# A chunked recurrence on one core: preparation in another order, and chunk products with a block-diagonal operand

## The chip, the cores and the metric

The kernel runs on one core of one Trainium2 chip. The metric is the device time of one execution in microseconds (us), less is better. The median of three runs of the kernel before is 684.5 us (683.43 to 689.24).

## What is computed

`reference` has two stages. The first is a recurrence over 768 steps t for each of 4 x 8 = 32 heads, with a 40 x 40 state S per head:

```
y_t = r_t S
S   = S * w_t  -  (S a_t) b_t^T  +  v_t k_t^T
```

(`w_t` scales the columns; all of r, k, v, w, a, b have 40 elements per head and step.) The second stage takes y, laid out as 4 x 768 x 320, through four causal attention experts of width 64, of which each token adds the two with the largest gate, weighted by a softmax over the two. The change touches the first stage alone.

## The kernel before, in words

**Chunks, units, windows.** The 768 steps are cut in 24 chunks of 32 steps. Heads are worked on eight at a time (a group g of 0 to 3), so a chunk has four *units* and the recurrence 96, `unit(u)` with u = 4 x chunk + g. Four chunks make a *window* (16 units, 128 steps), of which there are NW = 6. Each iteration n of the main loop issues one step of several units: `u` of unit n-1, `g` of n, `y` of n-3, `f` of n-2, `t` of n-6 (every second n), `k` on half of the iterations, `v` of n-1. Their matmuls run on TensorE (PE); ScalarE (ACT) brings most results out of PSUM; VectorE (DVE) applies the mask behind `f` (L398), multiplies the output y by the decay (L419), and for the last chunk of a window scales the state (L413, with the column PC). The state that `y` gives is read by `g` one iteration later, and the masked result of `f` by `y` of the next iteration.

**Preparation.** Before a window starts, each of its four groups needs `prep(i)`, i = 4 x window + g: two scans over the decays on DVE (`a`, L248, writes SUF; `s`, L254, writes SC), a reciprocal between them (`c`, L252), ScalarE's copy of four columns of SUF into PC (`b`, L250), the scaled a (`x`, L256, writes AA), the scaled k and b (`k` and `l` on DVE, L261, or `p` on GpSimd (POOL), L258, write KB), the products of AA and KB per chunk on PE (`m` for chunks 0 and 1, `n` for 2 and 3, L275), their masks on DVE (L278, into GL), two copies of AA into GL (`d`, `q`, L265 or L267), and a store of part of GL to DRAM (`o`, L282). `w`, `v`, `e` load the next group's inputs.

**Products.** One product is 40 rows of KB x 64 columns against 40 rows of AA x 32 columns, two heads at the array positions (0,0) and (64,64): 32 products per group.

**Inversion.** `invert(w)` loads the stored blocks (`L`), sets their diagonal (`C`), does 30 elimination steps of two instructions each (`T5` is five instructions; on POOL, L309, for window 0 a shorter form on DVE), and transposes (`A`, `B`, `D`, `E`, L311; `P`, L313). For window 0 the two halves are joined by matmuls (`F`, L320, and `H`, L328).

**What sets the order.** Every engine works its own instructions in program order, and that order is written by hand: `START` is the prologue, `EARLY` and the tables `SIDE`, `SIDE2`, `INV`, `INV1` say at which iteration, relative to the window's first, and at which slot (the number of slashes; three put a job behind `f`) which job is issued. Work for window W of `SIDE` is issued one to two windows ahead, -16 being the first iteration of window W-2. In the program before, groups 0 to 4 and the start of 5 are prepared in `START`, the rest of 5, and 6 and 7, in the first iterations of `EARLY`, and the groups of window 2 by `SIDE2` beside the units of window 0.

All PSUM tiles named `ps` come from one ring of four buffers that `u`, `g`, `f`, `v` and the products share.

Of the kernel before, what the change touches and what calls it, by code (L numbers as in the profile page):

```python
# [17 lines left out]
NW, NG, C = 6, 4, 32  # L18
NKB = 10

START = """Z0 E4 0abcsxkl E5 E7 E6 1apb 0m 0d 0q 0n 0o 1csx W2 2apb 1m 1d 1q 1n 1o W4 2csx 3apb 2m 2d 2q 2n 2o W0 W1 V00 V10
3csx 4apb 3m 3d 3q 3n 3o L W3 4csx W5 W6 5apbc 4m 4n C V01 V11 k0 g0 4o Z1 4d 4q T28 A B P F0 5s H0 5x 6apb"""
EARLY = {
    0: "///6cs",
    1: "5mno///6x 7apb/F1",
    2: "6mno///7csx/H1",
    3: "7mno E8",
    4: "/F2/5d/5q",
    5: "/H2/6d/6q",
    6: "/F3/7d/7q",  # L30
    7: "/H3",
}

SIDE = {
    -16: "///0abc",
    -15: "///0sx///0wv",
    -14: "///0k",
    -13: "///0l 1abc///0e",
    -12: "///0m 1s///1w",
    -11: "///1xkl///1ve",  # L40
    -10: "///2abc 1m",
    -9: "///2sx///2wv",
    -8: "///2kl///2e",
    -7: "///3abc 2m",
    -6: "///3sx///3wv",
    -5: "///3k",
    -4: "///3l 0ndqo///3e",
    -3: "///3m 1ndqo",
    -2: "///2ndqo",
    -1: "///3ndqo",  # L50
}

SIDE2 = {
    -13: "///0abc",
    -12: "///0sx///0wv",
    -11: "///0kl 1abc///0e",
    -10: "///1sx///1wv",
    -9: "///0m 1kl///1e",
    -8: "///2abc 1m",
    -7: "///2sxk///2wv",  # L60
    -6: "///2l 3abc///2e",
    -5: "///2m 3sx///3wv",
    -4: "///3kl 0ndqo///3e",
    -3: "///3m 1ndqo",
    -2: "///2ndqo",
    -1: "///3ndqo",
}
INV = {0: "L", 1: "C T5", 2: "T5", 3: "T5", 4: "T5", 5: "T5", 6: "T5", 7: "T5", 8: "T5", 9: "T5", 10: "T5///A", 11: "T5", 12: "T5", 14: "///D", 16: "E"}
INV1 = {4: "L", 5: "C T5", 6: "T5", 7: "T5", 8: "T5", 9: "T5", 10: "T5", 11: "T8", 12: "T8///A", 13: "T8", 14: "T8", 15: "///D", 16: "E"}


def layouts(r, k, v, w, a, b):
# [47 lines left out]
def recurrence(tc, ctx, I, xT, CM, early, tail=None):  # L120
    nc = tc.nc
    ep = early.enter_context(tc.tile_pool(name="early", bufs=1, side="right"))
# [3 lines left out]
    V, A, T, PL = nc.vector, nc.scalar, nc.tensor, nc.gpsimd  # L126
# [17 lines left out]
    SUF = ring("SUF", [104, 529], 1)[0]  # L144
    PC2 = ring("PC", [104, 2, 4], 6)
    SC2 = ring("SC", [104, 2, 16, 33], 6)
    PC, SC = ([t[k // 2][:, k % 2] for k in range(12)] for t in (PC2, SC2))
    KB = ring("KB", [128, 16, 64], NKB)
    AAr = [ep.tile([104, 16, 32], F32, name=f"AA{k}") for k in range(4)]
    GF = [ep.tile([128, 4098], F32, name="GLe")] + ring("GL", [128, 4098], 1)  # L150
    GL = [t[:, 0:4096].rearrange("p (g n s t) -> p g n s t", g=4, n=16, s=2) for t in GF]
    MT = ring("MT", [128, 32, 32], 2)
    RB1 = [ep.tile([128, 8, 32], F32, name=f"RB1{k}") for k in range(2)]
    P1 = ep.tile([128, 32, 16], F32, name="P1")
    EA7 = ep.tile([104, 512], F32, name="EA7")
# [8 lines left out]
    XT = ring("XT", [104, 8, 128], 2)  # L164
# [3 lines left out]
    flat = lambda t: t.rearrange("p a b -> p (a b)")  # L168
# [3 lines left out]
    own = (EWr[0], EAr[0], EKr[0])  # L172
    thirds = lambda t: (t[:, 0:528], t[:, 528:1040], t[:, 1040:2064])
    E8 = [own, thirds(r20), (flat(SC[11]), flat(LS[1])[:, 0:512], g1[:, 0:1024]), thirds(r21),
          (flat(SC[8]), flat(XT[1][:, 4:8]), flat(KB[8])), (flat(SC[9]), flat(XT[1][:, 0:4]), flat(KB[9])), own, (flat(SC[10]), EA7, flat(TT[1]))]

    SUFs = SUF, flat(TT[0])[0:104, 0:529]

# [33 lines left out]
    def rest(x):  # L212
# [19 lines left out]
        else:  # L232
            for k in range(2):
                for b in range(4):
                    q = slice(32 * b, 32 * b + 32)
                    A.activation(RB1[k][q, :, 16:32], ident[q, None, 32 * b + 16:32 * b + 32].to_broadcast([32, 8, 16]), AF.Copy)

    def prep(i):

        w, g = divmod(i, NG)  # L240
        aa, sc, kb, pc = AAr[i % 4], SC[i % 12], KB[i % NKB], PC[i % 12]
        gl = GL[w % 2]
        SUF = SUFs[1 if i in (1, 3, 5) else 0]
        sv = SUF[:, 1:529].rearrange("p (n c) -> p n c", c=33)
        EW, EA, EK = (x[0:104] for x in (E8[i] if i < 8 else own))
        ea = EA.rearrange("p (n c) -> p n c", c=32)
        def f0a():
            V.tensor_tensor_scan(SUF[:, 0:528][:, ::-1], EW[:, ::-1], d1[:, ::-1], 1.0, op0=OP.mult, op1=OP.add)  # L248
        def f0b():
            A.activation(pc, sv[:, ::4, 0], AF.Copy)  # L250
        def f0c():
            V.reciprocal(D1P[:, 0:528:132], sv[:, ::4, 0])  # L252
        def f1():
            V.tensor_tensor_scan(sc.rearrange("p n c -> p (n c)"), EW, D1P, 0.0, op0=OP.mult, op1=OP.add)  # L254
        def f2():
            V.tensor_tensor(aa, ea, sc[:, :, 0:32], op=OP.mult)  # L256
        def fp():
            PL.tensor_tensor(kb[0:104].rearrange("p n (k c) -> p n k c", k=2), EK.rearrange("p (n k c) -> p n k c", n=16, k=2),  # L258
                             sv[:, :, None, 1:33].to_broadcast([104, 16, 2, 32]), op=OP.mult)
        def fk(k):  # L260
            V.tensor_tensor(kb[0:104, :, 32 * k:32 * k + 32], EK.rearrange("p (n k c) -> p n k c", n=16, k=2)[:, :, k], sv[:, :, 1:33], op=OP.mult)  # L261
        def f5(s):
            o, x = gl[64:104, g, :, s, :], aa[64 * s:64 * s + 40]
            if i < 8:
                A.activation(o, x, AF.Copy)  # L265
            else:
                V.tensor_copy(o, x)  # L267
# [178 lines left out]
    P = [prep(i) for i in range(24)]  # L446
# [5 lines left out]
    for W in range(1, NW):  # L452
        n0 = 16 * (W - 1)
        inv = invert(W)
        for r, line in (SIDE if W != 2 else SIDE2).items():
            if W == 1:
                break
            for k, part in enumerate(line.split("/")):
                for z in part.split():
                    at(n0 + r, k, *[P[4 * W + int(z[0])][x] for x in z[1:]])  # L460
        for r, line in (INV1 if W == 1 else INV).items():
            for k, part in enumerate(line.split("/")):
                for z in part.split():
                    at(n0 + r, k, lambda z=z, inv=inv: inv[z[0]](*[int(x) for x in [z[1:]] if x]))
# [37 lines left out]
    for n in range(NU + 4):  # L502
# [468 lines left out]
```

## Time and profile before

| | |
|---|---|
| three runs, median (lowest to highest) | 684.5 us (683.43 to 689.24) |
| profiled execution | 682.19 us |
| its span, first to last instruction | 680.0 us |
| mean granted TensorE clock, share of full speed | 0.907 |
| busy: PE, DVE, ACT, POOL | 593.9, 493.1, 474.3, 321.0 us |
| recurrence (before the attention stage's own units) | about 430 of the 680 us |

A busy time counts an engine's instructions without its waits. Matmuls are pipelined, so PE's busy time is not PE at its peak. The span falls into stages that differ in what is late: a prologue in which few units run, four windows with preparation beside the units (0 to 3), two with little of it (4 and 5), and the attention stage. It is therefore read in stretches. A stretch ends here where the `f` matmuls of a unit start, since those of unit n-2 mark iteration n.

### The profile page before, as it was taken

To read this page: it belongs to the slowest core of one execution; us is meant where nothing else is said; L and a number is where in the kernel's file an instruction comes from. 1 tells how busy PE (TensorE), PEld (TensorE's weight loads), DVE (VectorE), ACT (ScalarE), POOL (GpSimd) and SP (SyncE) were. 2 spreads that over 40 slices of the span, in tenths; PEclk is the share of its full clock that TensorE was granted. 3 is DMA by queue.
4 is the path that set the end of the run, shared out by engine and by line. 5 is a ranking of instruction groups with operands and counts; after the bars stand their busy time and mean duration, and the time that the engine had idled before them with its cause. 6 is when DMAs were issued, how large, how long until landed. Compare 5 with 4: busy or idle time off the path is not lost. (4 is left out here: it accounts for less than half of the span.)

```text
span 680.0 us, 23382 instructions
## 1 busy us (share of the span) xinstructions
PE 593.9 (87%) x9361; PEld 514.6 (76%) x9361; DVE 493.1 (73%) x1164; ACT 474.3 (70%) x1295; POOL 321.0 (47%) x456
## 2 busy tenths in 40 slices
PE   5538797987997998889999989889899989999995
PEld 5527686976886887778988777778778877887774
DVE  7687458787887788788757776668887587667651
ACT  6892376666876786778899998457576666676762
POOL 2312089529925980797286020135555255343731
PEclk8555659788899799899999999989999999999998
DMA  7750445445655455653633882522131213202101
GB/s 240 221 124 11 105 126 120 103 119 151 153 128 157 129 135 115 181 131 87 174 97 83 259 211 69 165 56 73 56 92 35 78 32 83 65 11 57 40 30 46
DMA packets 63693, 73.90 MB, mean 109 GB/s; under 512 B 30168, under 2 KB 48344, under 8 KB 63576
## 3 DMA queue, kind: packets, MB, share of 16 engines
q1 hardware_dynamic: 63432, 72.21, 40.5%
q8 instruction: 77, 1.26, 0.8%
q14 instruction: 40, 0.33, 0.2%
q10 hardware_dynamic: 144, 0.10, 0.0%
HBM read 54.99 MB, written 11.01 MB: 97 GB/s over the span
## 5 line engine op out<-in xcount | busy, mean ns | idle before, releaser
L820 POOL TENSOR_TENSOR P<-P,m 128x128 f32<-128x128 f32 (+2 forms) x96 | 87.6, 934 | 95.3 <-DVE m L816 49.4
L309 POOL TENSOR_TENSOR MT<-MT,TP 128x30 f32<-128x30 f32 (+9 forms) x150 | 97.6, 651 | 11.8
L405 PE MATMUL py<-R,LS 128*40 128x80 f32 x1536 | 89.9, 246 | 14.9 <-ACT LS L435 9.7
L309 POOL TENSOR_TENSOR TP<-MT 128x30 f32<-128x30 f32 (+9 forms) x150 | 93.6, 624 | 11.4
L398 DVE TENSOR_TENSOR R<-ps,CM 64x128 f32<-64x128 f32 x192 | 55.1, 287 | 45.7 <-PE ps L395 42.2
L405 PEld LDWEIGHTS py<-R,LS 128*40 128x40 f32 x1536 | 67.4, 124 | 24.3 <-ACT LS L435 16.5
L809 ACT ACTIVATE P<-sc,m 128x128 f32<-128x128 f32 (+2 forms) x96 | 60.8, 634 | 29.9 <-DVE m L808 23.5
L275 PE MATMUL ps<-AA,KB 40*64 40x32 f32 x1536 | 64.2, 244 | 19.4 <-DVE AA L256 14.0
L275 PEld LDWEIGHTS ps<-AA,KB 40*64 40x64 f32 x1536 | 60.3, 164 | 23.0 <-issue 18.7
L808 DVE TENSOR_REDUCE m<-sc 128x1 f32<-128x128 f32 (+2 forms) x96 | 59.4, 622 | 20.1 <-PE sc L801 18.8
L798 PE MATMUL sc<-ks,qs 128*128 128x384 f32 (+4 forms) x256 | 62.5, 345 | 5.3 <-ACT P L809 5.1
L376 ACT ACTIVATE GT<-ps 32x160 f32<-32x160 f32 x192 | 56.4, 294 | 14.2 <-PE ps L373 10.8
L395 PE MATMUL ps<-RB,VU 128*64 128x64 f32 x768 | 49.3, 238 | 13.7 <-ACT VU L390 13.5
L384 ACT ACTIVATE R<-ps 32x160 f32<-32x160 f32 x192 | 56.6, 295 | 5.4 <-PE ps L382 1.2
L395 PEld LDWEIGHTS ps<-RB,VU 128*64 128x64 f32 x768 | 39.1, 148 | 19.5 <-ACT VU L390 18.5
L828 PE MATMUL pt<-CM,P 128*128 128x128 f32 x336 | 51.9, 276 | 2.1 <-ACT pt L834 1.8
L366 ACT ACTIVATE LS<-pt 64x320 f32<-64x320 f32 x96 | 41.4, 432 | 15.9 <-PE pt L362 14.5
L435 ACT ACTIVATE LS<-pt 40x320 f32<-40x320 f32 x92 | 39.6, 430 | 15.7 <-PE pt L431 12.6
L382 PE MATMUL ps<-GT,TT 128*33 128x80 f32 x768 | 48.8, 252 | 1.8 <-ACT GT L376 0.9
L798 PEld LDWEIGHTS sc<-ks,qs 128*128 128x128 f32 x256 | 40.8, 190 | 10.5 <-ACT P L809 9.4
L720 PE MATMUL pt<-xh,wq 128*128 128x384 f32 x192 | 43.3, 361 | 2.8 <-DVE pt L832 1.2
L431 PE MATMUL pt<-CM,R 104*104 104x104 f32 x368 | 44.6, 266 | 0.2 <-issue 0.2
(154 smaller groups left out, 1314.0 us busy)
## 6 DMA issues: line engine op xcount, KB each, us to landing
RB<-in_RB SPq DMA_DIRECT2D x24, 320.0 KB
EK<-in_EK SPq DMA_DIRECT2D x18, 416.0 KB
ks<-ks SPq DMA_DIRECT2D x32, 192.0 KB
R<-in_VG SPq DMA_DIRECT2D x24, 208.0 KB
EA<-in_EA SPq DMA_DIRECT2D x19, 208.0 KB
EW<-in_EA SPq DMA_DIRECT2D x18, 214.5 KB
R<-in_VT SPq DMA_DIRECT2D x48, 80.0 KB
R<-in_RT SPq DMA_DIRECT2D x24, 160.0 KB
```

The lines of the kernel that those rows point to most:

```text
L275: T.matmul(p_a[64 * s:64 * s + 64, p, cc - c], kb[q, n, :], aa[q, n, :], start=True, stop=True, tile_position=(64 * s, 64 * s))
L309: return [lambda: e.tensor_tensor(tmp, row, col, op=OP.mult), lambda: e.tensor_tensor(o, o, tmp, op=OP.add)]
L376: A.activation(gt[b:b + 32, s::2], p_g[64 * s:64 * s + 32], AF.Copy)
L384: A.activation(hd(r2[32:64, 40 * h0:40 * h0 + 320], 80)[:, x::2], p_u[64 * x:64 * x + 32], AF.Copy, scale=-1.0)
L395: T.matmul(p_f[64 * x:64 * x + 64, y], vu[:, p, :], rb[:, 4 * g + p, :], start=True, stop=True, tile_position=(0, 64 * x))
L398: V.tensor_tensor(o[:, :, x], p_f[64 * x:64 * x + 64], mask[x][:, None, None, :].to_broadcast([64, 2, 2, 32]), op=OP.mult)
L405: T.matmul(py[64 * s:64 * s + 40, p], ls[:, h, :], m, start=True, stop=True, tile_position=(0, 64 * s))
L798: T.matmul(ps[:, c, 0:cw], QS[b][:, e, o], KS[b][:, e, z, k], start=(z == 0), stop=(z == 1 and not last), skip_group_check=True)
L808: V.tensor_reduce(m[:, 0, t:t + 1], ps[:, 0:ch, 0:cw], axis=AX.XY, op=OP.max, negate=True)
L809: later(DE, lambda: A.activation(pv, ps[:, 0:ch, 0:cw], AF.Exp, bias=m[:, 0, t:t + 1], accum_out=m[:, 1, t:t + 1]))
L820: PL.tensor_tensor(P[:, 0:n], P[:, 0:n], m[:, 3, t:t + 1].to_broadcast([128, n]), op=OP.mult)
L828: T.transpose(p[:, 128 * y:128 * y + 128], st["P"][t][:, 128 * c:128 * c + 128], ident)
```

## The change

It does five things.

1. **Products.** AA [104, 16, 32] becomes AB [128, 16, 64], zero but for two blocks: the 32 columns of the first head of a pair in rows 0 to 39, those of the second in rows 64 to 103. One product takes 104 rows of KB x 64 columns against 104 rows x 64 columns of AB and gives both heads: 16 products per group, alternating between the array's column halves (0,0) and (0,64).
2. **`x`** becomes two instructions of 40 rows each, since the two blocks lie in different columns. The masks keep their number and size.
3. **`b`** is issued behind the scan `s` or later: in `SIDE` two iterations behind `a` of its group, where it stood directly behind `a`.
4. **`START`** prepares all of groups 0 to 7, and in it the masks of a group stand behind the scans of the next. `EARLY` keeps `F` and `H`. Window 2 uses `SIDE` and window 1 `INV`, so `SIDE2` and `INV1` go.
5. **`d`, `q`** of windows 2 to 5 move from the last four iterations of window W-2 to iterations 1, 3, 6 and 8 of window W-1. RB1, P1 and one staging area now lie in tiles that exist anyway; the four AB are set to zero at the start, one on DVE and three on POOL.

```diff
-START = """Z0 E4 0abcsxkl E5 E7 E6 1apb 0m 0d 0q 0n 0o 1csx W2 2apb 1m 1d 1q 1n 1o W4 2csx 3apb 2m 2d 2q 2n 2o W0 W1 V00 V10
-3csx 4apb 3m 3d 3q 3n 3o L W3 4csx W5 W6 5apbc 4m 4n C V01 V11 k0 g0 4o Z1 4d 4q T28 A B P F0 5s H0 5x 6apb"""
+START = """Z0 E4 0acsxklb E5 E7 E6 1acsxkl W2 0d 0q 1b 2ap 0mno 2csx W4 1d 1q 2b 3ap 1mno 3csx W0 2d 2q 4ap W1 3b 2mno 3mno L W3 V00 V10 3d 3q
+4csx W5 W6 5ap C 4b 4mno V01 V11 5csx Z1 4d 4q 6ap 5b 5mno k0 g0 6csx 5d 5q 7ap E8 6b 6mno 7csx T14 7mno 7b 6d 6q T14 A B P F0 H0 7d 7q"
 SIDE = {
-    -16: "///0abc",
-    -15: "///0sx///0wv",
...
+    -16: "///0ac",
+    -15: "///0s///0w",
+    -14: "///0bx///0v",
+    -13: "///0kl///0e",
+    -12: "///1acs///1w",
+    -11: "///1x 0m///1v",
...
+    -1: "///2no 3mno",
+    1: "///0dq",
+    3: "///1dq",
+    6: "///2dq",
+    8: "///3dq",
 }
...
+INV = {0: "L C T5", 1: "T5", 2: "T5", 3: "T5", 4: "T5", 5: "T5", 6: "T5", 7: "T5", 8: "T5", 9: "T5", 10: "T5///A", 11: "T5", 14: "///D", 16: "E"}
...
         def f2():
-            V.tensor_tensor(aa, ea, sc[:, :, 0:32], op=OP.mult)
+            for s in range(2):
+                q = slice(64 * s, 64 * s + 40)
+                V.tensor_tensor(ab[q, :, 32 * s:32 * s + 32], ea[q], sc[q, :, 0:32], op=OP.mult)
...
         def mm(c):
             p_a = ps([128, 4, 2, 32])
-            for n in range(16):
-                p, cc = divmod(n, 4)
-                if c <= cc < c + 2:
-                    for s in range(2):
-                        q = slice(64 * s, 64 * s + 40)
-                        T.matmul(p_a[64 * s:64 * s + 64, p, cc - c], kb[q, n, :], aa[q, n, :], start=True, stop=True, tile_position=(64 * s, 64 * s))
+            for p in range(4):
+                for x in range(2):
+                    n = p * 4 + c + x
+                    T.matmul(p_a[64 * x:64 * x + 64, p], kb[0:104, n, :], ab[0:104, n, :], start=True, stop=True, tile_position=(0, 64 * x))
```

On ScalarE, the copy PC for the third group of window 3. LS, VU, R and GT are what ScalarE brings out of PSUM for `k`/`t`, `v`, `u`/`y` and `g`. Before, in iteration 22, in which VectorE makes that group's scan `a`:

```order
L384 ACTIVATE R_128<-ps 32x2x80 x2
L376 ACTIVATE GT_137<-ps 32x4x40 x2
L415 ACTIVATE R_126<-py_78 40x4x40 x2
L250 ACTIVATE PC_87<-SUF_85 104x4
L435 ACTIVATE LS_124<-pt 40x8x40 x2
L390 ACTIVATE VU_130<-ps 80x256
```

The change, on the same engine, in iteration 25, two behind the one in which VectorE now makes that scan:

```order
L371 ACTIVATE R_123<-ps 32x2x80 x2
L363 ACTIVATE GT_132<-ps 32x4x40 x2
L402 ACTIVATE R_121<-py_77 40x4x40 x2
L237 ACTIVATE PC_87<-SUF_85 104x4
L353 ACTIVATE LS_119<-pt 64x320
L353 ACTIVATE LS_120<-pt 64x320
```

The copy has the same neighbours (a state copy ahead, an LS copy behind); what moved is the distance to the scan that it reads.

On VectorE in the prologue, groups 1 and 2 (scans, reciprocal, `x`, masks). Before:

```order
L248 SCALAR_TENSOR_TENSOR TT_121<-R_127,D_80 104x528
L278 TENSOR_TENSOR GLe<-ps,CM 64x4x2x32 x4
L252 RECIPROCAL D1P_84<-TT_121 104x4
L254 SCALAR_TENSOR_TENSOR SC_92<-R_127,D1P_84 104x528
L256 TENSOR_TENSOR AA_109<-R_127,SC_92 104x512
L248 SCALAR_TENSOR_TENSOR SUF_85<-SC_97,D_80 104x528
L278 TENSOR_TENSOR GLe<-ps,CM 64x4x2x32 x4
```

The change:

```order
L235 SCALAR_TENSOR_TENSOR TT_117<-R_123,D_80 104x528
L239 RECIPROCAL D1P_84<-TT_117 104x4
L241 SCALAR_TENSOR_TENSOR SC_92<-R_123,D1P_84 104x528
L245 TENSOR_TENSOR AB_109<-R_123,SC_92 40x16x32 x2
L250 TENSOR_TENSOR KB_99<-R_123,TT_117 104x16x32 x2
L235 SCALAR_TENSOR_TENSOR SUF_85<-SC_97,D_80 104x528
L265 TENSOR_TENSOR GLe<-ps,CM 64x4x64 x4
```

The masks of group 0 no longer stand between group 1's scans but behind all of group 1; `x` is two instructions.

## Rows read from the trace of the kernel before

**Rows 1.** Busy time by stretch: length, busy us (count) by engine, PE clock, DMA

```profile
0.00:52.36 52.36, 24.28 (x436) 23.33 (x437) 38.76 (x83) 41.81 (x54) 12.64 (x15) 0.63 0.68 190
52.36:141.23 88.87, 77.59 (x1813) 70.09 (x1813) 60.40 (x113) 48.86 (x146) 43.74 (x63) 0.70 0.41 96
141.23:204.92 63.69, 56.16 (x1188) 50.31 (x1184) 51.05 (x110) 46.64 (x141) 40.80 (x61) 0.92 0.55 138
204.92:267.88 62.96, 55.44 (x1188) 49.13 (x1184) 50.21 (x108) 46.65 (x141) 40.79 (x61) 0.95 0.56 140
267.88:330.30 62.42, 54.96 (x1188) 48.92 (x1184) 50.56 (x108) 46.65 (x141) 40.55 (x61) 0.95 0.51 127
330.30:372.33 42.03, 42.02 (x933) 37.22 (x929) 27.35 (x85) 38.70 (x113) 30.05 (x61) 1.00 0.42 117
```

**Rows 2.** Waits in 141.23 to 330.30: us in total, times, longest us

```profile
ACT PC L250 <- DVE SUF L248: 22.2, 12, 2.9
PE ps L395 <- ACT VU L390: 9.8, 11, 2.6
DVE R L398 <- PE ps L395: 20.3, 25, 2.2
DVE R L413 <- PE py L405: 6.1, 6, 1.9
```

**Rows 3.** Timeline, three engines: start us, us, instructions [idle before <-releaser]

```profile
219.46 0.21 ACT L250 ACTIVATE PC<-SUF 104x4 f32<-104x4 f32 x1 [2.39 <-DVE SUF L248]
221.01 0.45 PE L395 MATMUL ps<-RB,VU 128*64 128x64 f32 x8 [2.60 <-ACT VU L390]
221.51 0.59 DVE L398 TENSOR_TENSOR R<-ps,CM 64x128 f32<-64x128 f32 x2 [1.55 <-PE ps L395]
252.57 0.59 DVE L398 TENSOR_TENSOR R<-ps,CM 64x128 f32<-64x128 f32 x2 [0.58 <-PE ps L395]
```

**Rows 4.** Groups by form, 141.23 to 330.30: count | busy us, mean ns

```profile
L256 DVE TENSOR_TENSOR AA<-EA,SC 104x512 f32<-104x512 f32 x12 | 10.3, 856 | 0.4
L275 PE MATMUL ps<-AA,KB 40*64 40x32 f32 x768 | 26.9, 222 | 4.2 <-DVE KB L261 4.2
L395 PE MATMUL ps<-RB,VU 128*64 128x64 f32 x384 | 24.5, 237 | 9.8 <-ACT VU L390 9.8
```

**Rows 5.** Groups by form, whole span

```profile
L395 PEld LDWEIGHTS ps<-RB,VU 128*64 128x64 f32 x768 | 39.1, 148 | 19.5 <-ACT VU L390 18.5
L267 DVE COPY GL<-AA 40x512 f32<-40x512 f32 x16 | 6.9, 429 | 0.4
```

**Rows 6.** Timeline of the prologue, PE and DVE

```profile
7.68 1.28 DVE L261 TENSOR_TENSOR KB<-EK,SUF 104x512 f32<-104x512 f32 x2
23.03 3.63 PE L275 MATMUL ps<-AA,KB 40*64 40x32 f32 x64 [3.35 <-DVE AA L256]
24.98 0.88 DVE L278 TENSOR_TENSOR GLe<-ps,CM 64x256 f32<-64x256 f32 x2 [0.94 <-PE ps L275]
27.60 0.18 DVE L252 RECIPROCAL D1P<-TT 104x4 f32<-104x4 f32 x1
27.81 1.26 DVE L254 TENSOR_TENSOR_SCAN SC<-R,D1P 104x528 f32<-104x528 f32 x1
29.11 0.69 DVE L256 TENSOR_TENSOR AA<-R,SC 104x512 f32<-104x512 f32 x1
29.71 1.25 DVE L248 TENSOR_TENSOR_SCAN SUF<-SC,D 104x528 f32<-104x528 f32 x1
41.43 0.19 DVE L309 TENSOR_TENSOR TP<-MT 128x28 f32<-128x28 f32 x1
49.34 1.98 DVE L311 STREAM_TRANSPOSE TT<-MT 128x512 f32<-128x512 f32 x2
67.69 0.67 PE L395 MATMUL ps<-RB,VU 128*64 128x64 f32 x8
```

**Rows 7.** Waits in 52.36 to 141.23

```profile
DVE R L398 <- PE ps L395: 13.4, 9, 2.6
DVE GL L278 <- PE ps L275: 7.1, 5, 2.7
```

More of the change, by code (lines that the diff above doesn't have):

```diff
@@ L19 @@
 NKB = 10
-START = """Z0 E4 0abcsxkl E5 E7 E6 1apb 0m 0d 0q 0n 0o 1csx W2 2apb 1m 1d 1q 1n 1o W4 2csx 3apb 2m 2d 2q 2n 2o W0 W1 V00 V10
-3csx 4apb 3m 3d 3q 3n 3o L W3 4csx W5 W6 5apbc 4m 4n C V01 V11 k0 g0 4o Z1 4d 4q T28 A B P F0 5s H0 5x 6apb"""
+START = """Z0 E4 0acsxklb E5 E7 E6 1acsxkl W2 0d 0q 1b 2ap 0mno 2csx W4 1d 1q 2b 3ap 1mno 3csx W0 2d 2q 4ap W1 3b 2mno 3mno L W3 V00 V10 3d 3q
+4csx W5 W6 5ap C 4b 4mno V01 V11 5csx Z1 4d 4q 6ap 5b 5mno k0 g0 6csx 5d 5q 7ap E8 6b 6mno 7csx T14 7mno 7b 6d 6q T14 A B P F0 H0 7d 7q"""
@@ L23 @@
 EARLY = {
[L24 to L31, printed above, removed]
+    1: "////F1",
+    2: "////H1",
+    4: "////F2",
+    5: "////H2",
+    7: "////F3",
+    8: "////H3",
 }
 SIDE = {
-    -16: "///0abc",
-    -15: "///0sx///0wv",
[L37 to L50, printed above, removed]
-}
[L53 to L67, printed above, removed]
@@ L68 @@
-INV = {0: "L", 1: "C T5", 2: "T5", 3: "T5", 4: "T5", 5: "T5", 6: "T5", 7: "T5", 8: "T5", 9: "T5", 10: "T5///A", 11: "T5", 12: "T5", 14: "///D", 16: "E"}
-INV1 = {4: "L", 5: "C T5", 6: "T5", 7: "T5", 8: "T5", 9: "T5", 10: "T5", 11: "T8", 12: "T8///A", 13: "T8", 14: "T8", 15: "///D", 16: "E"}
+    -16: "///0ac",
[4 more added lines that the diff above has]
+    -11: "///1x 0m///1v",
+    -10: "///1bkl///1e",
+    -9: "///2ac 1m",
+    -8: "///2s///2w",
@@ L72, in layouts @@
+    -7: "///2bxk///2v",
+    -6: "///2l///2e",
+    -5: "///3ac 2m",
+    -4: "///3s 0no///3w",
+    -3: "///3bx 1no///3v",
+    -2: "///3kl///3e",
+    -1: "///2no 3mno",
[3 more added lines that the diff above has]
+    8: "///3dq",
+}
+INV = {0: "L C T5", 1: "T5", 2: "T5", 3: "T5", 4: "T5", 5: "T5", 6: "T5", 7: "T5", 8: "T5", 9: "T5", 10: "T5///A", 11: "T5", 14: "///D", 16: "E"}
 def layouts(r, k, v, w, a, b):
@@ L148, in recurrence @@
     KB = ring("KB", [128, 16, 64], NKB)
-    AAr = [ep.tile([104, 16, 32], F32, name=f"AA{k}") for k in range(4)]
+    ABr = [ep.tile([128, 16, 64], F32, name=f"AB{k}") for k in range(4)]
     GF = [ep.tile([128, 4098], F32, name="GLe")] + ring("GL", [128, 4098], 1)
@@ L152, in recurrence @@
     MT = ring("MT", [128, 32, 32], 2)
-    RB1 = [ep.tile([128, 8, 32], F32, name=f"RB1{k}") for k in range(2)]
-    P1 = ep.tile([128, 32, 16], F32, name="P1")
-    EA7 = ep.tile([104, 512], F32, name="EA7")
     TP = sp.tile([128, 240], F32, name="TP")
@@ L158, in recurrence @@
     TT = [t[:, 0:1024].rearrange("p (n t) -> p n t", n=32) for t in TF]
+    RB1 = [TT[1][:, 8 * k:8 * k + 8] for k in range(2)]
+    P1 = TT[1][:, 16:32].rearrange("k n t -> k (n t)").rearrange("k (n r) -> k n r", r=16)
     LS = ring("LS", [128, 32, 40], 2)
@@ L174, in recurrence @@
     E8 = [own, thirds(r20), (flat(SC[11]), flat(LS[1])[:, 0:512], g1[:, 0:1024]), thirds(r21),
-          (flat(SC[8]), flat(XT[1][:, 4:8]), flat(KB[8])), (flat(SC[9]), flat(XT[1][:, 0:4]), flat(KB[9])), own, (flat(SC[10]), EA7, flat(TT[1]))]
+          (flat(SC[8]), flat(XT[1][:, 4:8]), flat(KB[8])), (flat(SC[9]), flat(XT[1][:, 0:4]), flat(KB[9])), own, (flat(SC[10]), flat(LS[1])[:, 512:1024], flat(XT[0]))]
     SUFs = SUF, flat(TT[0])[0:104, 0:529]
@@ L201, in recurrence @@
     V.memset(D1P, 0.0)
+    V.memset(ABr[0], 0.0)
     for t in PY:
         V.memset(t[32:64], 0.0)
+    for t in ABr[1:]:
+        PL.memset(t, 0.0)
     for t in GF:
@@ L240, in prep @@
         w, g = divmod(i, NG)
-        aa, sc, kb, pc = AAr[i % 4], SC[i % 12], KB[i % NKB], PC[i % 12]
+        ab, sc, kb, pc = ABr[i % 4], SC[i % 12], KB[i % NKB], PC[i % 12]
         gl = GL[w % 2]
-        SUF = SUFs[1 if i in (1, 3, 5) else 0]
+        SUF = SUFs[1 if i in (1, 3, 5, 7) else 0]
         sv = SUF[:, 1:529].rearrange("p (n c) -> p n c", c=33)
@@ L262, in f5 @@
         def f5(s):
-            o, x = gl[64:104, g, :, s, :], aa[64 * s:64 * s + 40]
+            o, x = gl[64:104, g, :, s, :], ab[64 * s:64 * s + 40, :, 32 * s:32 * s + 32]
             if i < 8:
@@ L269, in mm @@
             p_a = ps([128, 4, 2, 32])
-            for n in range(16):
-                p, cc = divmod(n, 4)
-                if c <= cc < c + 2:
-                    for s in range(2):
-                        q = slice(64 * s, 64 * s + 40)
-                        T.matmul(p_a[64 * s:64 * s + 64, p, cc - c], kb[q, n, :], aa[q, n, :], start=True, stop=True, tile_position=(64 * s, 64 * s))
+            for p in range(4):
+                for x in range(2):
+                    n = p * 4 + c + x
+                    T.matmul(p_a[64 * x:64 * x + 64, p], kb[0:104, n, :], ab[0:104, n, :], start=True, stop=True, tile_position=(0, 64 * x))
             o = gl[0:64, g].rearrange("q (p c) s t -> q p c s t", p=4)
-            for s in range(2):
-                V.tensor_tensor(o[:, :, c:c + 2, s], p_a[64 * s:64 * s + 64], maskn[s][:, None, None, :].to_broadcast([64, 4, 2, 32]), op=OP.mult)
+            for x in range(2):
+                V.tensor_tensor(o[:, :, c + x], p_a[64 * x:64 * x + 64], maskn[x][:, None, None, :].to_broadcast([64, 4, 2, 32]), op=OP.mult)
         def f6():
@@ L454, in recurrence @@
         inv = invert(W)
-        for r, line in (SIDE if W != 2 else SIDE2).items():
+        for r, line in SIDE.items():
             if W == 1:
@@ L460, in recurrence @@
                     at(n0 + r, k, *[P[4 * W + int(z[0])][x] for x in z[1:]])
-        for r, line in (INV1 if W == 1 else INV).items():
+        for r, line in INV.items():
             for k, part in enumerate(line.split("/")):
```

## The prediction, as put on record before the changed kernel ran

> **What bounds the kernel now.** I read the busy time by stretch first [rows 1], then the waits of the stretch in which the change does most [rows 2], then one of these waits on three engines [rows 3], and last the prologue on the timeline [rows 6].
>
> The stretches show where time lies. From 330.30 to 372.33, sixteen iterations with nearly no preparation beside them, PE is busy 42.02 of 42.03 us: this is PE's own pace. The three stretches from 141.23 to 330.30 are sixteen iterations each with four groups of preparation, and take 63.69, 62.96 and 62.42 us, 189.1 in all; PE is busy for 55 to 56 of each, DVE for 50 to 51, ACT for 46.6 [rows 1]. No engine is full, so the 21 us above 42 are partly work and partly waits.
>
> The waits say which. ACT stands 22.2 us, 12 times, in front of the PC copy until DVE has made the scan SUF [rows 2]. Twelve is four groups in three windows: every group pays. The reader is to see in [rows 3] how one goes on: ACT waits 2.39 us for the scan, everything behind the copy in ACT's order (VU among it) is late, so PE stands 2.60 us before L395, and DVE, which had caused it, then waits 1.55 us for L395's result. All the PE waits of the three windows cost DVE 20.3 + 6.1 = 26.4 us [rows 2].
>
> The prologue is serial: PE stands 3.35 us until DVE has made AA, then takes 3.63 us for one group's products at the lower clock (the stretch's granted clock is 0.63, mostly 1.2 GHz), while DVE waits for its masks [rows 1, 6].
>
> **Preparation beside the units (141.23 to 330.30).**
>
> *The PC copy* itself stays, 0.21 us. Issued two iterations behind its scan, it finds SUF made. I take ACT's 22.2 us as gone, and ask what is late next.
>
> *DVE* is: of 189.1 us it is busy 51.05 + 50.21 + 50.56 = 151.8, and 37.3 are not busy, of which 26.4 are the waits above and 10.9 gaps between instructions and small waits [rows 1, 2]. The second `x` adds to it. No row shows a product of 40 rows x 512; the bounds are the copy of that shape, 0.43 us, and the product of 104 x 512, 0.86 [rows 4, 5]. I take 0.86, since the elements in a row are as many and it is the same operation: 12 x 0.86 = 10.3 us. Then DVE needs 151.8 + 10.3 + 10.9 = 173.0 us without any wait for PE, 57.7 per window, against 63.0 now. DVE is the new bound.
>
> *Its remaining waits.* Going through DVE's timeline from 204.92 to 267.88, waits like that of [rows 3] at 221.51, right behind a PC copy, make about two thirds of the L398 and L413 waits; those like the 0.58 us at 252.57, with no PC copy near, a third. A third of 26.4 is 8.8 us. A fuller DVE hides part of these, because PE and ACT run on while it works: bounds 0 and 8.8, I take 5.8, nearer to the upper end since PE still has to deliver `f` every iteration. Sum 178.8 us for the three windows: a gain of **10.3 us** (8.8 - 5.8 = 3.0 less at the upper bound, 5.8 more at the lower).
>
> *The products.* 768 records of 32 columns are 26.9 us of PE; the nearest row of the new form is L395, 64 columns on both operands, alternating column halves, 24.5 us for 384 records, and 384 is what the change leaves here [rows 4]. So 2.4 us, on an engine that is no longer last: I cost it at nothing. The cover is DVE's 57.7 us per window against about 42.0 + 24.5/3 = 50.2 on PE.
>
> *`d` and `q`* are moved, not added (8 x 0.43 = 3.4 us per window). Only the last of them enter the stretch from 330.30, where DVE is busy 27.35 of 42.03 us [rows 1]: nothing, 3.4 us if that slack could not be used. The load instructions on SP keep their order, `w` one iteration behind the scan that frees its buffer, and the next scan now comes three iterations behind it: nothing.
>
> **The prologue.** The order now lets PE's products of a group run under DVE's scans of the next, so DVE's own instructions are the sum. The first group's KB starts at 7.68; with a second `x` at 8.37, KB of groups 0 and 1 is 2.56 us more. For groups 1 to 7, `a`, `c`, `s` and two `x` are 1.25 + 0.18 + 1.26 + 2 x 0.69, about 4.2 us with the gaps, together 29.4. Masks are 8 x 1.76 and gaps, 14.4. The elimination takes 49.34 - 41.43 = 7.9, the transposes up to `F` 52.36 - 49.34 = 3.0 [rows 1, 6]. 8.4 + 2.6 + 29.4 + 14.4 + 7.9 + 3.0 = 65.7: `F` starts at about **65.7 us** instead of 52.36, 13.3 later, with 3 groups more prepared. ACT was busy 41.81 us there and gets some 4 us of `d` and `q` more; POOL loses group 1's KB and gains three memsets: both stay under it.
>
> **Window 0 (52.36 to 141.23, 88.87 us).** DVE is busy 60.40. Three groups leave it: five scans, three `x`, two `c` and twelve masks, 6.3 + 2.1 + 0.4 + 5.3 = 14.0 us, as do the four groups' `d`, `q`, 3.4; four second `x` come, 3.4. That leaves 46.4 busy. Of its 28.5 idle us, 13.4 + 7.1 = 20.5 are waits for PE [rows 7]; without these, and a load that it waited for, about 5 are gaps. To these come the run-in from `F` to the first L395, 15.3 us before [rows 6], of which two groups of products (7.3) go, so about 8, with 2.7 of DVE's own work in it: 5.3 idle. PE will enter at 1.2 GHz as before, and be the bound for some four iterations: about 5 us each, where DVE needs 3.4, so 6. With 2 for other waits: 46.4 + 5 + 5.3 + 6 + 2 = 64.7. The stretch ends at 65.7 + 64.7 = 130.4 instead of 141.23: a gain of **10.8 us**. Bounds: all 20.5 us of PE waits stay (72: 138), or the run-in alone (57: 122).
>
> **Sum.** The profiled execution took 682.19 us. 682.2 - 10.3 - 10.8 = **661 us**. The median of the runs shown, 684.5, lies 2.3 above the profiled one and their lowest 1.2 above; I do not add that. The attention stage is as before.
>
> **The rivals.**
>
> *Products that load their weights in the open.* The old products use two row halves of the array in turn, the new ones all rows. If each new one had to wait for its own load, 39.1/768 = 0.051 us [rows 5] would come to each of the 384 records, 24.5 + 19.6 = 44.1 us instead of 26.9, and PE would need 42.0 + 14.7 = 56.7 us per window, as much as DVE. Two full engines that wait for each other give the windows back: 682.2 - 10.8 = 671 us. Against it: L395 has this form already and shows 0.45 us for eight records [rows 3]. The Trainium skill, "TensorE: Matmul & The Clock Gate", Part 3, says that products with few rows should be put in different row groups, to run side by side, and that a load of weights overlaps a running matmul only where the row group differs; it speaks against this change. Chance 0.13.
>
> *Window 0 gives nothing.* The prologue is longer by 13.3 us for certain, and window 0 shortens only if PE leaves 1.2 GHz early. Its granted clock was 0.70 over the stretch [rows 1]; with the three groups' products gone PE has less to do there. If window 0 ends at 141 as before, only 10.3 us remain: 672. Chance 0.10.
>
> *Both of these*, or another wait that eats as much: about 682. Chance 0.07.
>
> *DVE becomes slower than PE was.* The `f` of an iteration uses a PSUM buffer that the products' masks must free, and the mask of `f` comes first in DVE's next iteration: if DVE's waits for PE came from this circle and not from the PC copy, all 26.4 us stay and the 10.3 us of `x` come on top. The windows would take 199.4 us, and with window 0 at its bad end (138, 3 gained) the time is 690. It decides at 16 us: if more than that of DVE's waits for PE is left in the three windows, they are slower than before. For it, that DVE waits for PE 25 times there and ACT for the scan only 12; against it, that the long ones follow the copies. Chance 0.05.
>
> *More than forecast.* DVE at 57.7 per window with nothing to wait for, and window 0 ended at 124: 682.2 - 16.1 - 17 = 649. Chance 0.15.
>
> **The numbers.** The forecast has 0.50; its own range is 654 to 668, by the bounds of the remaining waits and half of window 0's. From 648 to 677 it takes in the better case, the products' and window 0's, and leaves out the last two. A measurement of this kernel can tell about 1% (6.8 us) from no change, so faster means under 677.7: the forecast, the better case, and most of the two at 671 and 672, together 0.86. Within 1%: 0.09. Slower: 0.05.
>
> **What would show it.** In the changed profile ACT's wait for the scan is under 2 us in the windows; L245 shows 0.7 to 0.9 us per instruction; DVE's busy share in the windows is over 88% (before 80%); they take 58 to 61 us each; `F` starts at 64 to 67 us; iteration 16 starts near 130. I am wrong if DVE's waits for PE stay at about 9 us per window without a PC copy, if L262's 16 records of a half take much over 0.8 us, or if PE stays at 1.2 GHz through window 0.

## The result, and the profile after

The change made the kernel faster: **652.73 us** (median; 649.7 to 657.54) against 686.11 us for the kernel before in the same rounds, a ratio of **0.9519, interval 0.9443 to 0.9594**. The forecast was 661, from 648 to 677. Its sum was made against a profiled execution, so the traces are compared: 682.19 us before, 653.93 after, 28.3 less. One execution, of the kernel with the old products and the GpSimd copies, fell into a slower state of the chip and is left out of its time and ratio.

The same stretches as in [rows 1], of the kernel after: length, then busy us (and count) of PE, PEld, DVE, ACT and POOL, then granted clock, DMA share and GB/s. The first ends where `F` starts, the second with iteration 16, then come the three windows, then the next sixteen iterations.

```profile
0.00:67.01 67.01, 22.00 (x372) 20.27 (x373) 60.53 (x116) 44.85 (x60) 18.43 (x24) 0.62 0.73 175
67.01:129.26 62.25, 55.21 (x1493) 49.52 (x1494) 43.57 (x88) 46.68 (x141) 37.91 (x57) 0.84 0.44 104
129.26:186.80 57.54, 50.50 (x1062) 43.99 (x1059) 53.90 (x112) 46.65 (x141) 41.18 (x61) 0.97 0.62 153
186.80:244.47 57.67, 50.26 (x1062) 43.98 (x1059) 53.97 (x112) 46.64 (x141) 41.13 (x61) 0.97 0.61 151
244.47:301.55 57.08, 50.30 (x1062) 43.90 (x1059) 53.83 (x112) 46.64 (x141) 41.71 (x61) 0.97 0.57 143
301.55:343.55 42.00, 41.97 (x935) 37.24 (x930) 31.34 (x93) 38.16 (x112) 30.20 (x60) 1.00 0.42 117
```

The gain stands in two places. Iteration 16 starts at 129.26 instead of 141.23, 12.0 us earlier, although `F` starts 14.7 later. The three windows take 172.3 instead of 189.1 us, 16.8 less. The sixteen iterations behind them are as before, 42.00 against 42.03, though DVE does 4.0 us more there: in that stretch the moved `d` and `q` cost nothing.

In the windows DVE and PE have changed places. PE was busy for 55 to 56 us of each and now for about 50.3; DVE was busy for 50 to 51 and now for 53.9, which is 94% of a window's 57.4 us. All waits of ACT, and then all of DVE, between 129.26 and 301.55 (line waited for, us in total, times, longest):

```profile
ACT LS L353 <- PE pt L349: 15.4, 13, 3.1
ACT LS L422 <- PE pt L418: 6.6, 14, 0.8
ACT R L402 <- PE py L392: 1.0, 4, 0.3
ACT GT L363 <- PE ps L360: 0.8, 3, 0.3
```

```profile
DVE R L385 <- PE ps L382: 2.2, 3, 0.8
DVE R L400 <- PE py L392: 0.4, 2, 0.2
```

ACT's wait for the scan, 22.2 us in [rows 2], is gone. DVE's waits for the inputs of `f`'s mask (L385) and of the state's scaling (L400) are 2.2 + 0.4 us in place of 20.3 + 6.1. What ACT waits for now is PE. The groups by form of the same stretch, the answers to [rows 4] (count, busy us, mean ns, idle before):

```profile
L245 DVE TENSOR_TENSOR AB<-EA,SC 40x512 f32<-40x512 f32 x24 | 19.7, 823 | 0.5
L262 PE MATMUL ps<-AB,KB 104*64 104x64 f32 x384 | 15.8, 227 | 7.8 <-DVE KB L250 7.3 <-ACT R L371 0.5
L382 PE MATMUL ps<-RB,VU 128*64 128x64 f32 x384 | 23.0, 227 | 1.4 <-ACT VU L377 1.1
```

The halved `x` costs 0.82 us per instruction, nearly as much as one of 104 rows did (0.86). The products take 15.8 us of PE instead of 26.9. Single records overlap, so 0.227 us each is not their spacing; the timeline (start, us, instructions, wait) has sixteen of them in 0.69 us:

```profile
207.85 0.21 ACT L237 ACTIVATE PC<-SUF 104x4 f32<-104x4 f32 x1
212.70 0.69 PE L262 MATMUL ps<-AB,KB 104*64 104x64 f32 x16 [1.87 <-DVE KB L250]
```

The copy PC now stands on ACT with no wait ahead of it. A new wait is in the second row: PE comes to the products before DVE has made KB, 7.3 us in 6 waits in all.

### The profile page after: what moved, and what is told of

It reads as the page before. It is cut to its first block, busy times and chain, and to the rows that moved or that the text cites. A ratio compares the mean times of both kernels' runs of the same rounds, so it can differ in the third digit from the quotient of the medians.

```text
span 652.0 us, 21893 instructions
## 1 busy us (share of the span) xinstructions
PE 553.8 (85%) x8593; PEld 474.6 (73%) x8593; DVE 512.7 (79%) x1191; ACT 474.6 (73%) x1295; POOL 323.4 (50%) x458
## 5 line engine op out<-in xcount | busy, mean ns | idle before, releaser
L296 POOL TENSOR_TENSOR TP<-MT 128x30 f32<-128x30 f32 (+9 forms) x150 | 95.4, 636 | 11.4
L392 PE MATMUL py<-R,LS 128*40 128x80 f32 x1536 | 88.3, 241 | 6.3 <-DVE R L385 2.3
L385 DVE TENSOR_TENSOR R<-ps,CM 64x128 f32<-64x128 f32 x192 | 54.9, 286 | 31.3 <-PE ps L382 27.7
L392 PEld LDWEIGHTS py<-R,LS 128*40 128x40 f32 x1536 | 66.0, 121 | 16.0 <-ACT LS L422 7.6
L262 PE MATMUL ps<-AB,KB 104*64 104x64 f32 x768 | 35.9, 252 | 37.6 <-DVE AB L245 25.1
L262 PEld LDWEIGHTS ps<-AB,KB 104*64 104x64 f32 x768 | 32.0, 164 | 40.1 <-issue 30.5
L382 PE MATMUL ps<-RB,VU 128*64 128x64 f32 x768 | 46.6, 230 | 3.2 <-ACT VU L377 2.4
L785 PEld LDWEIGHTS sc<-ks,qs 128*128 128x128 f32 x256 | 40.8, 190 | 10.8 <-ACT P L796 9.7
L833 PE MATMUL ot<-pt,vv 128*64 128x256 f32 (+1 forms) x384 | 43.5, 359 | 0.0
```

The costliest lines, as they stand in the source:

```text
L262: T.matmul(p_a[64 * x:64 * x + 64, p], kb[0:104, n, :], ab[0:104, n, :], start=True, stop=True, tile_position=(0, 64 * x))
L296: return [lambda: e.tensor_tensor(tmp, row, col, op=OP.mult), lambda: e.tensor_tensor(o, o, tmp, op=OP.add)]
L385: V.tensor_tensor(o[:, :, x], p_f[64 * x:64 * x + 64], mask[x][:, None, None, :].to_broadcast([64, 2, 2, 32]), op=OP.mult)
L392: T.matmul(py[64 * s:64 * s + 40, p], ls[:, h, :], m, start=True, stop=True, tile_position=(0, 64 * s))
L785: T.matmul(ps[:, c, 0:cw], QS[b][:, e, o], KS[b][:, e, z, k], start=(z == 0), stop=(z == 1 and not last), skip_group_check=True)
L833: T.matmul(po[h, 128:256] if one else po[h], VV[b][:, k, 2 * ep + s], P[:, 256 * k:256 * k + (128 if one else 256)], start=(k == 0), stop= ...
```

## The experiments

The theory: the copy's late input and PE's share had been the limit; with the copy behind its scan DVE is the limit of the windows at its own pace, and the order of the prologue gives the rest. The rival: the copy is worth little by itself, and the new products carry the gain. Times are medians; each ratio is to the kernel before, run in the same rounds. Busy times and waits are from one profiled execution of each kernel.

**The copy alone.** The kernel before, `b` issued later, nothing else:

```diff
-    -16: "///0abc",
+    -16: "///0ac",
...
-    -14: "///0k",
+    -14: "///0bk",
```
(And so for the other groups, in `SIDE2` too.)

> The kernel before with one edit: ScalarE's copy PC two iterations behind its scan in the windows (old products, old prologue). Theory (the copy's wait stalled ScalarE, PE and then VectorE; VectorE's own work is the floor): ScalarE's wait for SUF falls from 22 us to under 3 in the three windows, which take 163 to 172 us instead of 189; window 0 some 4 us less; about 658 us in all. Rival 1 (the products did it): windows stay above 180 us, 675 us or more. Rival 2 (the order of masks and copies did it): the same, 675 us or more.

Measured: 666.26 us, ratio 0.9682 (0.9615 to 0.9748), 20.8 us less (16.6 between the two profiled executions, 682.19 and 665.59). The windows, and what DVE waits for in them:

```profile
139.62:198.96 59.34, 54.31 (x1188) 48.63 (x1184) 49.19 (x106) 45.56 (x138) 40.40 (x61) 0.94 0.61 145
198.96:256.21 57.25, 53.92 (x1188) 47.79 (x1184) 49.71 (x108) 46.64 (x141) 40.84 (x61) 0.97 0.63 153
256.21:313.56 57.35, 53.87 (x1188) 47.90 (x1184) 50.19 (x108) 46.65 (x141) 39.64 (x61) 0.97 0.57 139
```

```profile
DVE R L398 <- PE ps L395: 8.6, 9, 2.7
DVE KB L261 <- DMA EK<-in_EK: 4.5, 3, 2.0
DVE R L413 <- PE py L405: 1.9, 4, 1.0
DVE SUF L248 <- DMA EW<-in_EA: 1.4, 3, 0.7
```

One small instruction, moved past nothing but ACT's own work, takes 15.1 us out of the windows (189.1 to 173.9) with no operation removed, and DVE's waits for PE at these two lines fall from 26.4 to 10.5 us. A new wait, 4.5 us for EK to land, which DVE did not have in these windows before, takes a part of that back. It goes on to the other engines; in the first window:

```profile
159.29 1.94 DVE L261 TENSOR_TENSOR KB<-EK,SUF 104x512 f32<-104x512 f32 x2 [2.04 <-DMA EK<-in_EK]
161.37 1.92 PE L275 MATMUL ps<-AA,KB 40*64 40x32 f32 x32 [2.73 <-DVE KB L261]
163.00:167.00 4.00, 4.00 (x54) 3.77 (x54) 1.80 (x5) 2.01 (x6) 3.61 (x6) 0.50 0.89 218
167.63 0.61 DVE L398 TENSOR_TENSOR R<-ps,CM 64x128 f32<-64x128 f32 x2 [2.70 <-PE ps L395]
```

PE stands 2.73 us for KB, then works at 1.2 GHz (granted clock 0.50), and DVE in the end waits 2.70 us for it. The other two windows have the same order of events, with DVE's waits 1.67 and 1.36 us; together these are 5.7 of the 10.5 us that are left.

Iteration 16 starts at 139.62, 1.6 us earlier. Window 0 itself is 4.1 us shorter (84.75 for 88.87), but `F` starts 2.5 later, where DVE waits 2.5 us for a load that it did not wait for in the kernel before. So about 8 of the 12 us there belong to the rest of the change.

**The copy put back.** The changed kernel, `b` directly behind `a` again in `SIDE`:

```diff
-    -16: "///0ac",
+    -16: "///0abc",
...
-    -14: "///0bx///0v",
+    -14: "///0x///0v",
```
(And so for the other three groups.)

> The changed kernel with one edit undone: in the windows the copy PC directly behind its scan again. Theory: ScalarE waits 20 us or more for SUF again, the three windows go from 172 to 182 to 190 us, and the time from 653 to 662 to 672. Rival (VectorE is full, so ScalarE's wait hides behind it): windows below 176 us, time below 657.

Measured: 662.97 us, ratio 0.9629 (0.9565 to 0.9694), 10 us more than the change. One of the windows, and the waits from 127.75 to 310.70:

```profile
188.73:249.75 61.02, 50.29 (x1062) 43.72 (x1059) 54.27 (x112) 46.77 (x141) 40.55 (x61) 0.97 0.58 145
```

```profile
ACT PC L237 <- DVE SUF L235: 26.4, 12, 2.9
PE py L392 <- ACT LS L422: 13.5, 6, 3.0
PE ps L382 <- ACT VU L377: 7.5, 10, 1.2
DVE R L385 <- PE ps L382: 7.9, 15, 0.7
DVE R L400 <- PE py L392: 4.4, 3, 1.5
```

The whole chain of [rows 3] is back: twelve waits for the scan, PE late behind ACT, DVE late behind PE, with the same busy times as in the change. It costs 10.7 us in the windows (183.0 against 172.3) and nothing before them (iteration 16 at 127.75). The copy is worth 21 us in the old program and 10 in the new one; in the windows alone it is 15.1 and 10.7. With the copy directly behind its scan DVE waits 12.3 us for PE in the new program and 26.4 in the old one, so part of the same waits is already gone there. Which part of the change took them was not separated; the parts do not add up.

**The old products under the new order.** The changed kernel with AA, one `x` and 32 products of 40 rows (tiles, memsets and the masks' slices follow, not shown):

```diff
-            for s in range(2):
-                q = slice(64 * s, 64 * s + 40)
-                V.tensor_tensor(ab[q, :, 32 * s:32 * s + 32], ea[q], sc[q, :, 0:32], op=OP.mult)
+            V.tensor_tensor(aa, ea, sc[:, :, 0:32], op=OP.mult)
...
-                    T.matmul(p_a[64 * x:64 * x + 64, p], kb[0:104, n, :], ab[0:104, n, :], start=True, stop=True, tile_position=(0, 64 * x))
+                        T.matmul(p_a[64 * s:64 * s + 64, p, cc - c], kb[q, n, :], aa[q, n, :], start=True, stop=True, tile_position=(64 * s, 64 * s))
```

> The changed kernel with the old products: 32 of 40 rows per group, one scaling instruction of 104 rows, no zero blocks. Theory (VectorE is the bound in prologue and windows, PE is not): VectorE loses 12 x 0.85 = 10 us in the three windows, 3 in window 0, 5.5 in the prologue; windows 162 to 166 us, time 635 to 642, so the new products cost time. Rival (the products on PE brought part of the gain): windows 172 us or more, time 653 or more.

Measured: 656.92 us (651.4 to 658.21), ratio 0.9545 (0.948 to 0.961): not to be told from the change. The theory had this kernel clearly faster, since DVE loses the second `x`, and that part of it **fell**. The prologue, window 0 and one of the three windows, and DVE's waits for PE in the three:

```profile
0.00:64.80 64.80, 35.07 (x629) 33.80 (x629) 53.57 (x107) 44.63 (x60) 15.94 (x21) 0.60 0.69 182
64.80:130.49 65.69, 58.81 (x1620) 53.49 (x1622) 41.54 (x86) 47.28 (x143) 36.38 (x57) 0.85 0.44 103
186.55:242.77 56.22, 52.30 (x1188) 46.36 (x1185) 51.11 (x107) 46.88 (x141) 39.86 (x61) 1.00 0.61 157
```

```profile
DVE R L382 <- PE ps L379: 6.0, 9, 0.9
DVE R L397 <- PE py L389: 3.1, 5, 1.9
```

DVE is 2.8 us lighter in a window, but the window is only about 1.4 us shorter (168.2 against 172.3 for the three): PE is busy 52.3 of its 56.2 us at full clock, and DVE's waits for PE are back at 6.0 + 3.1 us. In the prologue PE is busy 35 us instead of 22, and `F` starts 2.2 earlier where DVE has 7 us less to do. Window 0 then takes 3.4 us longer, but that difference is not firm: the next kernel, with the same products, has 62.55 us there, and the change has 62.25 and, profiled a second time, 59.76. The new products buy room on PE with work on DVE, and as far as these times tell the two cancel in this program.

**The old products, `d` and `q` on GpSimd.** As the last one, and the two copies of groups 8 and up go from DVE to POOL, back into the last four iterations of the window before:

```diff
-                V.tensor_copy(o, x)
+                PL.tensor_copy(o, x)
```

> As the kernel with the old products, and the copies d and q of windows 2 to 5 on GpSimd at the end of the window before, where it stands idle. Theory: VectorE loses another 4 us per window, windows 152 to 158 us unless ScalarE (49 us per window) or PE (51) comes last; time 625 to 635. Rival (GpSimd's copies are long and delay the elimination, or slow VectorE beside them): windows no shorter than with the old products alone, 637 us or more.

Measured: 650.12 us (646.38 to 651.14), ratio 0.942 (0.9331 to 0.951); the theory's time was missed by 15 us, and the result is in the rival's range. The second of the three windows, and DVE's wait over it and the third:

```profile
186.29:242.51 56.22, 52.18 (x1188) 46.39 (x1186) 45.83 (x100) 47.69 (x144) 43.57 (x67) 1.00 0.66 158
```

```profile
DVE R L378 <- PE ps L375: 11.3, 16, 1.4
```

DVE is 5 us lighter than with the old products alone and the window exactly as long: DVE waits for PE instead. The third takes 55.3 us, the first 59.0, with a granted clock of 0.91 and PE busy 56.0 us of it. With the old products, then, the pace is not DVE's; PE is busy for 93 to 95% of each window. The rival's own reason (copies that are long on GpSimd) is not what the trace shows: DVE's waits there are for PE.

**The change once more, in a second set of rounds**, as the base for the next three:

> The changed kernel once more, as the measure for the three beside it on one chip: windows near 172 us, time 650 to 658.

Measured: 653.01 us, ratio 0.9485 (0.9434 to 0.9536); windows 171.7 us, in which DVE is busy 162.2 and waits 1.5 for PE. Iteration 16 starts at 127.06 here and at 129.26 in the first profile of the same kernel, so a difference of 2 us there is no finding.

**More work on DVE.** The change, with the first of the two `x` done twice from window 2 on (the second time to the same effect):

```diff
-            for s in range(2):
+            for s in (0, 1) if i < 8 else (0, 0, 1):
```

> The changed kernel with the first half of the scaling x issued twice for the groups of windows 2 to 5, the same values written again: one more VectorE instruction of 0.85 us per group. Theory (VectorE has no slack left in the windows): one for one, 12 x 0.85 = 10 us in the three windows (181 to 183 us), 2 to 3 us in window 0, time 11 to 14 us above the changed kernel. Rival (VectorE has slack, as the small gain from taking work away suggests): windows 175 to 178 us, time 3 to 6 us above.

Measured: 666.25 us, ratio 0.9681 (0.9615 to 0.9747), 13.2 us more than the change. One of the windows:

```profile
189.49:250.91 61.42, 53.06 (x1062) 45.80 (x1058) 56.70 (x116) 46.74 (x141) 42.15 (x61) 0.94 0.59 143
```

```profile
DVE R L385 <- PE ps L382: 5.8, 6, 1.6
```

Twelve more instructions of 0.82 us are 9.8 us; DVE's busy time in the windows grows by 7.8, its waits for PE by 4.3 (5.8 for 1.5, over the three windows), and the windows by 12.4 (184.1 against 171.7). With the new products every microsecond on DVE is paid, and a little more, in waits for a PE whose granted clock is 0.94 here and was 0.97 to 1.00. Had there been slack, as the run of the old products let one suspect, the time would not have moved.

**Less work on DVE.** The change with `d` and `q` on GpSimd, as two experiments above:

> The changed kernel (new products), with the copies d and q of windows 2 to 5 on GpSimd at the end of the window before. Theory (VectorE sets the windows of the changed kernel, and the room that the new products make on PE shows only once VectorE is relieved): VectorE's busy time per window falls from 53.9 to about 49 us, the three windows take 160 to 165 us instead of 172 and fewer than the 168 of the variant with old products, time 8 to 11 us below the changed kernel. Rival (a chain of ScalarE and PE sets a floor of 56 us per window, whatever the products): windows 166 to 169 us, time 3 to 5 us below the changed kernel.

Measured: 642.66 us (639.08 to 645.28), ratio 0.933 (0.9278 to 0.9381), 10.4 us less than the change. One of the windows:

```profile
183.43:238.43 55.00, 50.63 (x1062) 44.19 (x1059) 49.84 (x104) 46.65 (x141) 47.89 (x72) 0.97 0.66 157
```

```profile
DVE R L381 <- PE ps L378: 5.5, 8, 1.5
```

The windows take 164.0 us, 7.7 less. DVE is 12.1 us lighter in them; 4.0 of that come back as waits for PE (5.5 for 1.5). With the old products the same relief gave 59.0, 56.2 and 55.3 us; here two windows take 55.0 and 55.2 and one 53.8. The room that the new products make on PE shows only once DVE is relieved too. This kernel is faster than the change and than the kernel before; against the last one with the old products the intervals overlap. The edit moves the copies to another engine and to other iterations at once, and which of the two counts was not tried.

**And one product later.** As the last, with `m` of the second group an iteration later, behind the KB that PE waited for in the change:

```diff
-    -9: "///2ac 1m",
+    -9: "///2ac",
...
-    -8: "///2s///2w",
+    -8: "///2s 1m///2w",
```

> As the changed kernel with the copies on GpSimd, and the second group's products m one iteration later, since PE stands 1.9 us in each window until VectorE has made their KB. Theory (that stand is on the path): windows 1 to 2 us shorter each, 156 to 162 us in all, time 3 to 5 us below the variant without it. Rival (it is hidden behind VectorE or ScalarE): the same within 1 us per window.

Measured: 641.10 us (639.33 to 644.6), ratio 0.9326 (0.9274 to 0.9378). One of the windows, and what is left of DVE's waits for PE in the three:

```profile
180.11:232.98 52.87, 48.99 (x1062) 42.57 (x1059) 49.17 (x104) 46.66 (x141) 47.76 (x68) 1.00 0.73 166
```

```profile
DVE R L381 <- PE ps L378: 0.8, 2, 0.4
```

In the traces the windows are 4.2 us shorter (159.8), and the granted clock is 1.00 in all three where it was 0.97 in two. The times of the two kernels overlap, so whether the step is worth anything is open. Its reason had gone, too: in the last kernel's trace PE no longer waits for that KB, and the longest waits of PE there are for VU (4.4 us in 3), which stay as they were.

## Why the prediction was right

The time fell in the stated range, but below the 654 that bounded the forecast itself: it lies between the forecast and the case "more than forecast". The windows, too, came out under the 58 to 61 us that were named as a sign.

**The bound.** It said that DVE would be the limit of the windows, and DVE is: without `d` and `q` (12.1 us) the windows shrink by 7.7, with 9.8 us more they grow by 12.4. DVE's busy time was forecast at 151.8 + 10.3 = 162.1 us and came to 161.7. The second `x` was priced by the 104-row product, 0.86; it takes 0.82, and in the prologue, where the 104-row one took 0.69 [rows 6], it takes 0.69 as well, so the number of elements in a row set the cost here and not the number of rows. That the totals agree to 0.4 us is in part luck. The copies `d` and `q`, put at nothing, cost 13.8 us for 24 of them in the windows where 26 cost 11.1 before (the last section has the reason), and the rest of DVE's busy time came out lower.

**The windows** gained 16.8 us, not 10.3. The mechanism held and two terms were mis-sized: the remaining waits for PE, taken as 5.8 us, are 2.6, near the lower bound; and the gaps, taken over as 10.9, are 8.0. With DVE's 0.4 that is the whole of 178.8 - 172.3 = 6.5. The gaps were too large because 26.4 us were not all of DVE's waits for PE. The masks of the products waited as well, 3.3 us, and the prediction counted these as gaps that stay. In the change they are gone. Before:

```profile
DVE GL L278 <- PE ps L275: 1.9, 4, 0.5
DVE GLe L278 <- PE ps L275: 1.4, 2, 1.0
```

The choice of 5.8, toward the upper end, rested on PE having to deliver `f` in each iteration. It does, but from a PE that has 5 us less to do per window and so is ahead of DVE. Waits like the 0.58 us of [rows 3], with no PC copy near, were taken as the measure of what stays. With the old products DVE's waits for PE are 10.5 us when the copy alone is moved and 9.1 under the new order, about the 8.8 that this measure gives; with the new ones they are 2.6. The products are a part of that: with them and DVE about as light (busy 150.1 us in the kernel with `d` and `q` on GpSimd, 149.1 and 152.7 in those two) the waits are 5.5. The rest may go with DVE's own load, as the prediction argued, but no run holds all else equal.

Not all of the old waits were of the kind that it named. The longest one in the window that it read, 2.18 us, ends at 227.77, 8 us behind the nearest PC copy, while PE works at 1.2 GHz (eight matmuls of L395 take 0.64 us at 227.09, where they take 0.45 in [rows 3]). With the copy alone moved, one such wait in each window is left, behind PE's stand for KB; in the change they are 0.6 to 0.85 us.

**Products at nothing.** Hidden under DVE they are, and they are also cheaper than forecast: 15.8 us and not 24.5. In the change that room is worth nothing clear of noise beyond the second `x` (the run with the old products is not to be told from it); it is worth something with DVE relieved.

**The prologue and window 0.** `F` starts at 67.0 us for 65.7, 1.3 later than summed. Window 0 took 62.3 for 64.7, since DVE is busy 43.6 us in it where the sum had 46.4, and iteration 16 starts at 129.3 for 130.4: 12.0 us gained for 10.8. Two small errors cancel here, and the larger is no more than the 2.5 us between two profiles of the change (62.3 and 59.8). In the runs with the copy put back and with the old products iteration 16 starts at 127.8 and 130.5, with the copy alone at 139.6. So this part belongs in the main to the rest of the change, the new order of prologue and preparation; no run tries the order of `START` or the move of `d` and `q` by itself.

**The rivals.** Loading weights in the open did not come: PE's busy time in the products fell by 11.1 us where this rival had it rise by 17.2. The rule that spoke for it, that small products go side by side in different row groups and a load overlaps only where the row group differs (the Trainium skill, "TensorE: Matmul & The Clock Gate", Part 3), is not borne out by this shape: sixteen products over all rows take 0.69 us, loads included. The granted clock of window 0 rose from 0.70 to 0.84 (0.85 with the old products), and the window ended 12 us earlier, so the rival in which it gives nothing was wrong as well. The circle through PSUM that would have made the windows slower needed 16 us of waits for PE; there are 2.6. The case "more than forecast", 649 us, described the windows best (172.3 against its 173.0), while window 0 ended where the forecast had it.

Of the two large terms, then, the copy's is the one that the runs isolate: alone it is worth 21 us.

## What to carry to other kernels

An engine that works in order pays for an instruction that is issued too early with everything behind it: look for short instructions with a long wait on an engine that is far from full, and move them down until their input is ready, before anything is made cheaper. When the bound goes to another engine, take its busy time plus its gaps as the floor, and look in its waits for the old bound for those that go with it: here all but 2.6 of 26.4 us went, but with the old products 9 to 10 stayed. A change that takes work from one engine and gives some to another is worth what the engine that is last then gains: price it again whenever the other is relieved.

## What was not expected of the hardware

In window 0 of the change PE stands still in the middle of sixty-four small matmuls, for nothing that the profile shows. The change, then the one with the old products:

```profile
88.95 0.32 PE L315 MATMUL ps<-TT,TT 32*32 32x16 f32 x17 [2.97 <-issue]
```

```profile
86.86 0.44 PE L312 MATMUL ps<-TT,TT 32*32 32x16 f32 x33 [2.58 <-issue]
```

In the change, with the copy put back, with more work on DVE, and in both kernels with the new products and the GpSimd copies it falls at the same instruction, with 17 of the 64 to go, and takes 1.9 to 3.6 us. With the old products, a program with more instructions ahead of that place, it falls at another, with 33 to go. So its place follows the program. With the old products and the GpSimd copies the sixty-four part at the same instruction as in the second row, without a wait worth naming. What PE waits for there was not tried, and the cause stays open. The granted clock falls behind it; the stretch with the wait, and one that begins 4.6 us after its end, in the change:

```profile
85.00:88.90 3.90, 0.98 (x64) 0.83 (x59) 3.76 (x7) 1.18 (x4) 3.67 (x4) 1.00 0.71 131
93.50:97.20 3.70, 3.70 (x50) 3.54 (x51) 2.48 (x5) 2.44 (x8) 3.39 (x5) 0.50 0.39 80
```

From full speed, 2.4 GHz, PE goes to 1.2 GHz (0.50) after those 3.9 us in which it was busy for 0.98, and eight matmuls of L382 take 0.64 us at 92.74 where they take 0.40 at 97.40.

DVE's copy of 40 x 512 slows down beside GpSimd. Two pairs in one window of the change on DVE, and GpSimd at the second (at the first it stands, until 194.61):

```profile
192.27 0.86 DVE L256 COPY GL<-AB 40x512 f32<-40x512 f32 x2
198.54 1.21 DVE L256 COPY GL<-AB 40x512 f32<-40x512 f32 x2
```

```profile
198.48 0.41 POOL L296 TENSOR_TENSOR TP<-MT 128x130 f32<-128x130 f32 x1
198.97 0.50 POOL L296 TENSOR_TENSOR MT<-MT,TP 128x130 f32<-128x130 f32 x1
```

The first pair takes 0.43 us each, which was the mean in the kernel before [rows 5], the second 0.60. It is the same in the other windows (0.86 at 134.73 and 249.93 with GpSimd idle, 1.20 to 1.21 at 140.88 and 256.09 with it at work). AB's layout is not the cause: from AA, under the new order, the copy takes 0.57 to 0.59 on average over the run. So the move of `d` and `q` to where GpSimd eliminates made them dearer. On GpSimd itself the copy takes 0.66 us:

```profile
238.63 5.29 POOL L247 COPY GLe<-AA 40x512 f32<-40x512 f32 x8
```
